# Attention with a linear memory, then an FFN: half-height causal masks for sequence 0, a parametric ReLU in the weight decode, ln(256) as the bias of the exponential, and three tiny preparation steps on ScalarE

## The chip, the cores and the metric

The kernel runs on one core of a Trainium2 chip (trn2). The metric is device time in microseconds (us): the median of the runs. Engines are named as in the profile: PE is TensorE's matmul stream and PEld its weight loads, DVE is VectorE, ACT is ScalarE, POOL is GpSimd, SP is SyncE, which issues the DMAs.

## What is computed

Eight sequences (B) of 576 tokens with eight heads of width 64 go through causal attention, which is mixed by a gate with a read from a per-head memory; the result, 4608 rows of 512, goes through a feed-forward block (FFN).

```python
scores = where(causal, -1e9, q @ k.T / sqrt(64));  a = exp(scores - scores.max(-1))
local  = (a / (a.sum(-1) + 1e-9)) @ v
q_p    = where(q > 0, q, exp(q) - 1) + 1
mem    = (q_p @ M_prev) / (q_p @ z_prev + 1e-6)
x      = sigmoid(beta) * mem + (1 - sigmoid(beta)) * local      # -> [4608, 512]
h      = x @ w_in                                               # w_in  [512, 2048], float64
out    = (h * clip(h + 3, 0, 6) / 6) @ w_out                    # w_out [2048, 512], float64
```

q, k, v, the memory and the gate are float32, both FFN weights float64.

## The kernel before

**Number formats.** From sequence 1 on every operand is split into two float16 parts (hi and lo), scaled by powers of two; a product is then three float16 matmuls (two for the scores, where the parts of k are stacked on the partitions). Sequence 0 and the first FFN block of 256 tokens have no time for that preparation and use float32 matmuls ("natural" operands, `nat`). The profile shows a float32 matmul as two passes.

**Attention.** A unit is one head and one group of 128-query blocks: block 0 and 1, block 2, block 3, or block 4 (64 rows). 256 units, eight sequences of 32. Scores stand with keys on the partitions in one PSUM bank. Per unit: the score products (L343 float32 for sequence 0, with the 64 dimensions of one head on 64 partitions: 0 to 63 for the first head of a pair, 64 to 127 for the second; L347 and L348 float16), and for the diagonal block one more product that adds the causal mask: identity (float16, 128 rows) times a matrix of 0 and -3e38 (L350). Then the maximum over key blocks (L360, or a copy on ACT, L358), the maximum over the partitions on POOL (L362), the subtraction on DVE (L368), the exponential on ACT (L377), and from sequence 1 on the float16 parts (L381 on POOL, L389 on DVE). Two units later come the products with v and with the memory (L407 and L408 in float32; L413 to L417), then their combination (L430 to L438).

L368 is a scalar_tensor_tensor: scores plus a shift, minus the maximum. The shift is such that the exponential comes out times 256. For sequence 0 it is a number, otherwise a column of 128 numbers (`scal[:, 1:2]`) read from SBUF.

**Preparation.** Ten steps per pair of heads (28 pairs, sequences 1 to 7) load q, k, v, find the largest sums of magnitudes (ACT L152, POOL L186), turn them into scales (`scale()`, L188 to L202, all of it on DVE) and split and stack the operands (ACT L156, DVE L157, DMAs).

**Weights.** The float64 words of the FFN weights are decoded by integer operations in 16 jobs of 128 x 1024 (L622 to L626): the upper word, read as float32 and scaled, goes through ACT; DVE shifts left by 3 (L623), puts the sign bit back from the upper word (L624), and adds three bits from the lower word (L625); ACT sums magnitudes. The first eight jobs are `w_in`, the rest `w_out`.

**FFN.** 18 blocks of 16 pieces: eight pieces of the first product (L523 to L525, float32 for block 0: L518), with the activation (L531 to L534), and eight of the second (L546 to L548, float32: L544). A piece is wanted at a time counted in pieces; attention is given priorities some pieces ahead. `nc` is built with a scheduler that orders all instructions of an engine by these priorities and by its own estimate of time. So the order on each engine is fixed when the program is built, and an edit of one step can move others.

Each engine runs its instructions in order; only the weight loads of PE go ahead.

Of the kernel before, what the change touches and what calls it, by code (L numbers as in the profile page):

```python
# [12 lines left out]
F32 = mybir.dt.float32  # L13
F16 = mybir.dt.float16
BF16 = mybir.dt.bfloat16
# [3 lines left out]
ALU = mybir.AluOpType  # L19
# [4 lines left out]
P = 128  # L24
EXP_BITS = 0x7F800000
TS = 14          # operands are scaled so that the largest sum of magnitudes along a row is in [2^TS, 2^(TS+1))
TF = 8           # weights are scaled so that the largest magnitude is in [2^TF, 2^(TF+1))
TG = 2.0 ** -9   # g is kept as TG * S * g
SA = 256.0       # exp() values are kept times SA
TINY = 2.0 ** -40  # L30
NSLOT = 6        # pairs of heads whose operands are on chip
NNAT = 1         # blocks of the FFN whose products are float32 ones
# the order of emission, in units of the attention, and the pieces of the FFN that things are wanted at
X_T = 10         # the first unit after which pieces of the FFN follow
SPL_K = 4        # parts of the second weights that are split per piece of the FFN
W_T = [9] * 8 + [10, 10, 11, 11, 12, 12, 13, 13]
PSS, PSO = 3, 2
# first loads: 0, 1 are the parts of a pair's q, k and v, 2 a job of the weights, 3 the memory
LOADS = ((0, 0), (3, 0), (0, 1), (0, 2), (0, 3), (2, 0), (2, 1), (1, 0), (1, 1), (2, 2), (1, 2), (1, 3), (2, 3))
B_T = (2, 3, 4, 5)  # L40
OF = (0,)        # query blocks of sequence 0 whose products stand in the FFN's banks
RMAX_STEPS = 3.0
LEAD = 40        # attention runs so many pieces of the FFN ahead
LEAD0 = 10
PO = 8           # preparation comes so many pieces after the unit that it is emitted at
XL = 12          # x comes so many pieces before the products that are emitted with it
DW = (-20, 2, 0, 1)      # decoding of the weights: first and step, for each of them
S1 = 8           # their splits
S2 = (16, 0.25)
TAIL = 80        # pieces of the FFN that are left to the end  # L50
HLB = 3
XPB = 4
# when the steps of preparing the pairs of the next sequence come, in units of this one
# [14 lines left out]
def kernel(ctx, tc, qT, kT, v, mz, beta, w_in, w_out, out):  # L68
    nc = tc.nc
    PE, DVE, ACT, POOL, SP = nc.tensor, nc.vector, nc.scalar, nc.gpsimd, nc.sync  # L70
    B, NP, _, S = qT.shape          # 8, 4, 128, 576
    H = 2 * NP
    D = 64
    NT, DM = out.shape              # 4608, 512
    DFF = w_in.shape[1]             # 2048
    NB = 5                          # 128-token tiles per sequence (the last one has 64)
    TB = 256                        # tokens of an FFN block
# [39 lines left out]
    for i in range(NSLOT):  # L117
        sizes = [2 * NB * P, 4 * S, 2 * S, NB * 2 * 129]
        whole = const.tile([P, sum(sizes) + 2], F16, name=f"slot{i}")
        at = 0  # L120
        for lst, n, pat, kw in zip((kst, qhl, qps, vst), sizes,
                                   ["p (h s) -> p h s", "p (x h s) -> p x h s", "p (h s) -> p h s",
                                    "p (t h e) -> p t h e"],
                                   [dict(h=2), dict(x=2, h=2), dict(h=2), dict(t=NB, h=2)]):
            lst.append(whole[:, at:at + n].rearrange(pat, **kw))
            at += n
        if i < NP:
            w32 = whole.bitcast(F32)
            nat.append(dict(q=w32[:, 0:S], k=w32[:, S:S + NB * P], qp=w32[:, S + NB * P:2 * S + NB * P],
                            v=w32[:, 2 * S + NB * P:2 * S + NB * P + NB * 130]  # L130
                            .rearrange("p (t h e) -> p t h e", t=NB, h=2)))
        else:
            raw.append(whole[:, 0:4096])

    def at(step):
        """what follows is wanted when so many pieces of the FFN are done"""
        tc.cur_priority = int(round(step * 1000))

    def scales(am, n, t, tag):
        """Power-of-two scales s, and 1/s, that bring each column's largest value to [2^t, 2^(t+1))."""  # L140
# [13 lines left out]
    def split(hi, lo, src, s):  # L154
        """hi + lo = src * s, both float16."""
# [4 lines left out]
    slots = {}  # L160

    def prep_steps(b, p):
# [25 lines left out]
        def scale():  # L188
            amr = st["amr"]
            DVE.tensor_scalar_add(amr[:, 3:4], amr[:, 0:1], 1.0)  # L190
# [4 lines left out]
            DVE.tensor_scalar(scal[:, 1:2], s[:, 0:1], s[:, 1:2], 8.0 * LN_SA, op0=ALU.mult, op1=ALU.mult)  # L195
            DVE.memset(scal[:, 2:3], SA * 1e-9)
            DVE.tensor_scalar(scal[:, 3:4], s[:, 3:4], 1e-6, mem[b]["s"][:, 1:2], op0=ALU.mult, op1=ALU.mult)
            coef = mem[b]["coef"][:, 2 * p:2 * p + 2]
            DVE.tensor_scalar_mul(coef[:, :, 0], omg[:, 2 * p:2 * p + 2], i[:, 2:3])
            eps = scal[:, 2:4].unsqueeze(1).broadcast_to([P, 2, 2])  # L200
            esc, shift = scal[:, 0:1], scal[:, 1:2]
            slots[b, p] = dict(sl=sl, esc=esc, shift=shift, coef=coef, eps=eps)  # L202
# [43 lines left out]
    def nat_load(p, part):  # L246
        """a pair of heads of sequence 0, for float32 products"""
# [12 lines left out]
    def nat_phi(p, part):  # L260
# [6 lines left out]
        slots[0, p] = dict(esc=0.125, shift=8.0 * LN_SA, coef=coef,  # L267
# [15 lines left out]
    def mem_steps(b):  # L283
# [16 lines left out]
        def conv():  # L300
# [7 lines left out]
            mem[b] = dict(t=t, s=s, coef=coef)  # L308
# [4 lines left out]
    # a unit: some 128-query blocks of one head, their scores in one PSUM bank, keys on partitions  # L313
# [4 lines left out]
    class Unit:  # L318
# [11 lines left out]
        def scores(self):  # L330
# [6 lines left out]
            for i, nq, c0, _ in self.blocks:  # L337
                q0 = i * P
                for j in range(i + 1):
# [9 lines left out]
                    if j == i:  # L349
# [14 lines left out]
        def sub(self):  # L364
            a = self.a = p2.tile([P, 512], F32, name=f"a_{self.id}", tag="a")
            for i, nq, c0, m0 in self.blocks:
                w = (i + 1) * nq
                DVE.scalar_tensor_tensor(  # L368
                    a[:, c0:c0 + w].rearrange("p (t q) -> p t q", q=nq),
                    self.sT[:, c0:c0 + w].rearrange("p (t q) -> p t q", q=nq),  # L370
                    slots[self.b, self.p]["shift"],
                    self.mb[:, m0:m0 + nq].unsqueeze(1).broadcast_to([P, i + 1, nq]),
                    op0=ALU.add, op1=ALU.subtract)

        def exp(self):
            a = self.a[:, 0:self.n]
            ACT.activation(a, a, AF.Exp, scale=slots[self.b, self.p]["esc"])  # L377
# [68 lines left out]
    # a block of TB tokens: the parts of x tiles that it holds  # L446
# [33 lines left out]
    def x_split(n, most):  # L480
        """float16 parts of x, for as many parts of block n as there are tiles for them"""
# [75 lines left out]
    ffn_pos = [0, 0]        # block, piece  # L557
    x_pos = [0, 0]          # next block to be transposed, its next step

    def x_step():  # L560
        """one step of bringing x of the next block into place; True when there was one to do"""
# [4 lines left out]
        free = n == fn or fk >= 8      # the tiles that the products of the block before read  # L566
# [32 lines left out]
    def w_raw(n):  # L599
        """where the words of job n stand: in the place of the other weights, or of what comes later"""  # L600
# [13 lines left out]
    def w_decode(n):  # L614
        """float64 chunks c and c + 1, as pairs of words, to float32 in chunks c + 1 and c + 2 of W"""
# [5 lines left out]
        # as a float32, the upper word has the upper 8 bits of the exponent, and the lower 3 in its fraction  # L621
        ACT.activation(m, hi.bitcast(F32), AF.Copy, scale=2.0 ** -112)  # L622
        DVE.tensor_single_scalar(d, d, 3, op=ALU.logical_shift_left)  # L623
        DVE.scalar_tensor_tensor(d, hi, -0x80000000, d, op0=ALU.bitwise_and, op1=ALU.bitwise_or)  # L624
# [36 lines left out]
    DVE.tensor_copy(negm, negf)  # L661
    DVE.memset(bias_g, TG / 2.0)
# [43 lines left out]
    def due(t):  # L706
        """the piece of the FFN that comes at the time of unit t"""
# [101 lines left out]
```

## Time and profile before

| | us |
|---|---|
| median of 3 runs | 1117.56 |
| fastest, slowest of the 3 | 1116.35, 1119.19 |
| span of the profiled execution | 1120.2 |
| PE busy in it | 1083.2 |
| DVE busy | 930.7 |
| ACT busy | 791.1 |
| POOL busy | 412.2 |

The profiled execution is a further one; the page gives its span, from its first to its last instruction, and no other time for it. The span is 2.6 us above the median and 1.0 above the slowest of the three.

How to read it: a group row has the line, engine and operation, out<-in, shapes and count, then busy us and mean ns of one, then the idle time of the engine just before them and what ended it. A timeline row has its start, how long it took, engine, line, operation, and how many were merged. Matmuls overlap in their pipeline, so a row's length is a latency; the time that one occupies PE is the distance between starts.

### The profile page before, as it was taken

Reading aid. Unit: us, or ns where it says so; the run is one execution under the profiler, and the core shown is the slowest. Engines: PE = TensorE matmul, PEld = TensorE weight load, DVE = VectorE, ACT = ScalarE, POOL = GpSimd, SP = SyncE. Lnnn points to the kernel's source line nnn. Section 1 sums busy time; section 2 is a strip of 40 time slices with the busy share of each in tenths; the row PEclk is TensorE's granted clock in tenths of the full one; section 3 lists DMA queues with packets and bytes.
Section 4 is the critical chain, followed back from the end, with each engine's and each line's share of the span. In section 5 each row is a group of like instructions: output and inputs, shape, how many; then the busy total and the mean of one; then the engine's idle time right before and its main releaser. Section 6 shows DMA issues by size and latency. Waiting matters only on the chain.

```text
span 1120.2 us, 28768 instructions
## 1 busy us (share of the span) xinstructions
PE 1083.2 (97%) x10736; PEld 797.4 (71%) x10736; DVE 930.7 (83%) x2436; ACT 791.1 (71%) x1880; POOL 412.2 (37%) x544
## 2 busy tenths in 40 slices
PE   8999999999999899999999999999999999999998
PEld 6888767586767667676768576867685868685664
DVE  5999889899899969998999988888799968893321
ACT  5787879677877778787877787668686857563321
POOL 3322223444444433554244533354344433341000
PEclk9999999999999999999999999999999999999999
DMA  8734452333424343315332434233404230101100
GB/s 263 291 100 160 119 135 70 94 91 87 116 84 106 70 118 89 97 45 138 97 76 71 101 96 102 76 92 97 116 22 107 77 69 14 36 5 36 27 13 19
DMA packets 101468, 101.39 MB, mean 91 GB/s; under 512 B 50256, under 2 KB 80976, under 8 KB 101328
## 3 DMA queue, kind: packets, MB, share of 16 engines
q1 hardware_dynamic: 101328, 99.56, 33.1%
q8 instruction: 84, 1.38, 0.5%
q14 instruction: 56, 0.46, 0.1%
HBM read 48.14 MB, written 9.44 MB: 51 GB/s over the span
## 4 chain that ended last, share of the span: by engine, by line
PE 42%; DVE 32%; ACT 8%; issue 8%; DMA 6%; POOL 2%; SPq 1%; DVEq 0%; ACTq 0%; POOLq 0%
DVE a L368 6%; PE po L546 5%; PE po L548 5%; PE po L547 5%; PE ph L523 5%; DVE rm L360 5%; PE ph L524 4%; PE ph L525 4%; DVE al L389 4%; DVE r L532 3%; PE ph L518 3%; DVE g L534 2%; PE sT L343 2%; DVE W L157 2%; POOL mb L362 2%
## 5 line engine op out<-in xcount | busy, mean ns | idle before, releaser
L362 POOL PARTITION_ALL_REDUCE mb<-rm x256 | 251.7, 983 | 336.7 <-DVE rm L360 237.4
L523 PE MATMUL ph<-x,W 128*128 128x256 f16 x1088 | 297.6, 274 | 12.7 <-DVE r L532 7.3
L525 PE MATMUL ph<-x,W 128*128 128x256 f16 x1088 | 297.5, 273 | 0.0
L524 PE MATMUL ph<-x,W 128*128 128x256 f16 x1088 | 297.4, 273 | 0.0
L381 POOL TENSOR_SCALAR_AFFINE_SELECT ah<-a 128x384 f16<-128x384 f32 (+2 forms) x224 | 145.4, 650 | 214.4 <-ACT a L377 105.4
L546 PE MATMUL po<-W,g 128*128 128x512 f16 x544 | 206.6, 380 | 1.9 <-ACT ot L554 1.6
L548 PE MATMUL po<-W,g 128*128 128x512 f16 x544 | 206.5, 380 | 0.8 <-DVE g L534 0.8
L547 PE MATMUL po<-W,g 128*128 128x512 f16 x544 | 206.7, 380 | 0.0
L377 ACT ACTIVATE a<-a,scal 128x384 f32<-128x384 f32 (+2 forms) x224 | 141.6, 633 | 57.0 <-DVE a L368 48.8
L368 DVE SCALAR_TENSOR_TENSOR a<-sT,scal,mb 128x128 f32<-128x128 f32 (+4 forms) x280 | 147.2, 541 | 13.3 <-POOL mb L362 12.4
L360 DVE TENSOR_REDUCE rm<-sT 128x128 f32<-128x256 f32 (+3 forms) x256 | 135.6, 530 | 11.5 <-PE sT L350 4.6
L389 DVE TENSOR_TENSOR al<-a,ah 128x384 f16<-128x384 f32 (+2 forms) x224 | 134.0, 598 | 9.2 <-POOL ah L381 8.0
L532 DVE SCALAR_TENSOR_TENSOR r<-r,ph 128x512 f32<-128x512 f32 x136 | 92.1, 677 | 53.2 <-ACT r L531 52.6
L436 ACT ACTIVATE x<-o,cf 128x64 f32<-128x64 f32 (+1 forms) x320 | 100.6, 314 | 44.2 <-DVE cf L432 39.5
L531 ACT ACTIVATE r<-ph,bias_g,gsc 128x512 f32<-128x512 f32 x136 | 106.5, 783 | 34.2 <-PE ph L525 29.1
L347 PE MATMUL sT<-slot 128*128 128x128 f16 (+1 forms) x840 | 123.7, 210 | 3.9 <-DVE a L368 2.1
L348 PE MATMUL sT<-slot 128*128 128x128 f16 (+1 forms) x840 | 124.3, 210 | 0.0
L523 PEld LDWEIGHTS <-W 128*128 128x128 f16 x1088 | 106.8, 98 | 23.1 <-issue 6.6
L413 PE MATMUL o<-slot,ah 128*128 128x65 f16 (+1 forms) x840 | 116.3, 195 | 6.9 <-ACT y L437 3.6
L533 ACT ACTIVATE g<-r 128x512 f16<-128x512 f32 x136 | 86.4, 636 | 51.2 <-DVE r L532 51.1
L524 PEld LDWEIGHTS <-W 128*128 128x128 f16 x1088 | 106.7, 98 | 19.5 <-issue 5.0
L414 PE MATMUL o<-slot,ah 128*128 128x64 f16 (+1 forms) x840 | 115.4, 195 | 0.0
(149 smaller groups left out, 2387.4 us busy)
## 6 DMA issues: line engine op xcount, KB each, us to landing
slot<-q SPq DMA_DIRECT2D x112, 144.0 KB, 2.5
out<-ot SPq DMA_DIRECT2D x36, 256.0 KB, 2.0
stv<-vn SPq DMA_DIRECT2D x28, 320.0 KB, 3.3
W<-w_in SPq DMA_DIRECT2D x8, 1024.0 KB, 9.5
slot<-w_out SPq DMA_DIRECT2D x8, 1024.0 KB, 4.9
stq<-qT SPq DMA_DIRECT2D x28, 288.0 KB, 3.1
stk<-kT SPq DMA_DIRECT2D x28, 288.0 KB, 3.3
slot<-k SPq DMA_DIRECT2D x112, 72.0 KB, 2.0
```

The source lines that it names most:

```text
L360: DVE.tensor_reduce(rm[:, m0:m0 + nq], src.rearrange("p (t q) -> p q t", q=nq), axis=AX.X, op=ALU.max)
L362: POOL.partition_all_reduce(mb[:, 0:self.m], rm[:, 0:self.m], P, RMAX)
L368: DVE.scalar_tensor_tensor(a[:, c0:c0 + w].rearrange("p (t q) -> p t q", q=nq), self.sT[:, c0:c0 + w].rearrange("p (t q) -> p t q", q=nq), ...
L377: ACT.activation(a, a, AF.Exp, scale=slots[self.b, self.p]["esc"])
L381: POOL.affine_select(self.ah[:, 0:self.n], a, pattern=[[0, self.n]], compare_op=ALU.is_ge, fill=0.0, base=1, channel_multiplier=0)
L389: DVE.tensor_tensor(self.al[:, 0:n], self.a[:, 0:n], self.ah[:, 0:n], op=ALU.subtract)
L523: PE.matmul(ph[:, m], wh, f["xh"][:, c], start=c == 0, stop=False)
L524: PE.matmul(ph[:, m], wh, f["xl"][:, c], start=False, stop=False)
L525: PE.matmul(ph[:, m], wl, f["xh"][:, c], start=False, stop=c == 3)
L546: PE.matmul(po, gh[:, m, ts], W2[:, m, 0:512], start=m == 0, stop=False)
L547: PE.matmul(po, gh[:, m, ts], W2[:, m, 512:], start=False, stop=False)
L548: PE.matmul(po, gl[:, m, ts], W2[:, m, 0:512], start=False, stop=m == 15)
```

## The change

Comments are dropped as well, so lines move: what was L343, L350, L368, L377 and L624 to L625 stands in the new file at L349, L357, L378, L385 and L633 (the old L624 is gone). Five things change:

1. **Masks of sequence 0.** In place of one product of 128 rows and 128 columns there are two (one in the 64-row block) of 64 rows and 64 columns, on the same 64 partitions as the head's score products. Their operands, `selm` and `neg2`, lie in the unused end of an operand slot and are built at the start by some 15 small DVE instructions. Sequences 1 to 7 keep the old mask.
2. **Subtraction.** L368 becomes a tensor_tensor: scores minus maximum, without the shift.
3. **Exponential.** ln(256) is the bias of the activation. In the built program the bias was the number 0.0 and is the number 5.545; no operand is added.
4. **Decode.** Instead of a copy the activation is a parametric ReLU whose slope for negative inputs is -2^32: after the shift left by 3 the sign bit is then in place, and L624 goes.
5. **Tiny steps.** Of the nine instructions of `scale()` on 1 to 4 columns, one goes (the shift), and three move from DVE to ACT: q's sum plus 1, the scaled epsilon, and a coefficient. A column `eps1` per sequence is added (DVE).

```diff
+            selm = free[:, 0:2 * P].rearrange("p (a k) -> p a k", a=2)
+            neg2 = free[:, 2 * P:3 * P].rearrange("p (a q) -> p a q", a=2)
...
         def scale():
-            DVE.tensor_scalar_add(amr[:, 3:4], amr[:, 0:1], 1.0)
+            ACT.activation(amr[:, 3:4], amr[:, 0:1], AF.Copy, bias=1.0)
             s, i = scales(amr, 4, TS, f"{b}_{p}")
...
-            DVE.tensor_scalar(scal[:, 1:2], s[:, 0:1], s[:, 1:2], 8.0 * LN_SA, op0=ALU.mult, op1=ALU.mult)
             DVE.memset(scal[:, 2:3], SA * 1e-9)
-            DVE.tensor_scalar(scal[:, 3:4], s[:, 3:4], 1e-6, mem[b]["s"][:, 1:2], op0=ALU.mult, op1=ALU.mult)
+            ACT.activation(scal[:, 3:4], s[:, 3:4], AF.Copy, scale=mem[b]["eps1"])
-            DVE.tensor_scalar_mul(coef[:, :, 0], omg[:, 2 * p:2 * p + 2], i[:, 2:3])
+            ACT.activation(coef[:, :, 0], omg[:, 2 * p:2 * p + 2], AF.Copy, scale=i[:, 2:3])
...
-                    if j == i:
+                    if j == i and self.b == 0:
+                        for a in range(nq // D):
+                            PE.matmul(o[:, a * D:(a + 1) * D], selm[r, a, :], neg2[r, a, :],
+                                      start=False, stop=a == nq // D - 1)
+                    elif j == i:
                         PE.matmul(o, ident16, negm[:, 0:nq], start=False, stop=True)
...
-                DVE.scalar_tensor_tensor(
+                DVE.tensor_tensor(
                     a[:, c0:c0 + w].rearrange("p (t q) -> p t q", q=nq),
                     self.sT[:, c0:c0 + w].rearrange("p (t q) -> p t q", q=nq),
-                    slots[self.b, self.p]["shift"],
-                    self.mb[:, m0:m0 + nq].unsqueeze(1).broadcast_to([P, i + 1, nq]),
-                    op0=ALU.add, op1=ALU.subtract)
+                    self.mb[:, m0:m0 + nq].unsqueeze(1).broadcast_to([P, i + 1, nq]), op=ALU.subtract)
...
-            ACT.activation(a, a, AF.Exp, scale=slots[self.b, self.p]["esc"])
+            ACT.activation(a, a, AF.Exp, scale=slots[self.b, self.p]["esc"], bias=LN_SA)
...
-        ACT.activation(m, hi.bitcast(F32), AF.Copy, scale=2.0 ** -112)
+        ACT.activation(m, hi.bitcast(F32), AF.Prelu, scale=2.0 ** -112, alpha=-2.0 ** 32)
         DVE.tensor_single_scalar(d, d, 3, op=ALU.logical_shift_left)
-        DVE.scalar_tensor_tensor(d, hi, -0x80000000, d, op0=ALU.bitwise_and, op1=ALU.bitwise_or)
         DVE.scalar_tensor_tensor(d, lo, 29, d, op0=ALU.logical_shift_right, op1=ALU.bitwise_or)
```

The scheduler makes another order of it on every engine. Three places follow. First PE at the start of the program, the scores of sequence 0, heads 0 and 1 of the first pair; `sT` is a unit's PSUM bank (sequence, group, pair and head are left out of some names, a number at the end counts buffers), `slot_102` that pair's q and k, `ident` and `negm` the mask's operands. Before:

```order
L343 MATMUL sT_0_0_0_191<-slot_102 128x128
L350 LDWEIGHTS ident_89
L350 MATMUL sT_0_0_0_191<-negm,ident_89 128x128
L343 MATMUL sT_0_0_0_191<-slot_102 128x128 x2
L350 LDWEIGHTS ident_89
L350 MATMUL sT_0_0_0_191<-negm,ident_89 128x128
L343 MATMUL sT_0_0_1_206<-slot_102 128x128
```

And now, with `slot_105` for the place of `selm` and `neg2`:

```order
L349 MATMUL sT_0_0_0_206<-slot_102 128x128
L357 LDWEIGHTS slot_105
L357 MATMUL sT_0_0_0_206<-slot_105 128x64
L357 LDWEIGHTS slot_105
L357 MATMUL sT_0_0_0_206<-slot_105 128x64
L349 MATMUL sT_0_0_0_206<-slot_102 128x128 x2
L357 LDWEIGHTS slot_105
L357 MATMUL sT_0_0_0_206<-slot_105 128x64
L357 LDWEIGHTS slot_105
L357 MATMUL sT_0_0_0_206<-slot_105 128x64
L349 MATMUL sT_0_0_1_223<-slot_102 128x128
```

The units stand in the same order; each mask has become two weight loads and two products of half the columns. Over the whole order the masks of sequence 0 are 40 products before and 72 now, and PE changes between 64-row and 128-row products 97 times before and 63 times now.

Second DVE, the second decode job and the attention around it; `W_95` holds the decoded words, `W_96` the raw ones, `cf`, `rm`, `a` and `slot` belong to attention. Before:

```order
L430 TENSOR_TENSOR cf_0_0_1_0_285<-o_0_0_0_0_237,nat_eps 128x4
L625 SCALAR_TENSOR_TENSOR W_95<-W_96,W_95 128x1024
L623 TENSOR_SCALAR W_95<-W_95 128x1024
L430 TENSOR_TENSOR cf_0_0_1_1_296<-o_0_0_0_1_240,nat_eps 128x4
L431 RECIPROCAL cf_0_0_1_0_285<-cf_0_0_1_0_285 128x4
L265 SCALAR_TENSOR_TENSOR slot_102<-slot_102 128x320
L624 SCALAR_TENSOR_TENSOR W_95<-W_96,W_95 128x1024
L431 RECIPROCAL cf_0_0_1_1_296<-cf_0_0_1_1_296 128x4
```

And now:

```order
L438 TENSOR_TENSOR cf_0_0_1_0_310<-o_0_0_0_0_258,nat_eps 128x4
L632 TENSOR_SCALAR W_95<-W_95 128x1024
L439 RECIPROCAL cf_0_0_1_0_310<-cf_0_0_1_0_310 128x4
L438 TENSOR_TENSOR cf_0_0_1_1_321<-o_0_0_0_1_261,nat_eps 128x4
L633 SCALAR_TENSOR_TENSOR W_95<-W_96,W_95 128x1024
L440 TENSOR_TENSOR cf_0_0_1_0_310<-cf_0_0_1_0_310,coef_161 128x4
```

A job is two DVE instructions instead of three, and the small steps of attention (`cf`) stand behind one long instruction less.

Third the scales of pair 0 of sequence 1. On DVE before (`amr` are the reduced sums, `i` and `s` the scales, `wi` belongs to the weights):

```order
L144 TENSOR_SCALAR i_0_694<-i_0_694 128x4
L143 TENSOR_SCALAR i_wi<-wm_i 128x1
L145 RECIPROCAL s_0_693<-i_0_694 128x4
L194 SCALAR_TENSOR_TENSOR scal_0_698<-i_0_694 128x1
L199 TENSOR_SCALAR coef_262<-omg,i_0_694 128x2
L196 MEMSET scal_1_959 128x1
L195 TENSOR_SCALAR scal_0_698<-s_0_693 128x1
L197 TENSOR_SCALAR scal_0_698<-s_0_693,s_m_252 128x1
```

And now on ACT, with attention (`a`, `r`) and the weights (`W`, and `slot_106` and `slot_107` as their scratch) between:

```order
L195 ACTIVATE amr_0_674<-amr_0_674 128x1
L385 ACTIVATE a_1_3_0_833<-a_1_3_0_833 128x384
L631 ACTIVATE W_96<-slot_107 128x1024
L634 ACTIVATE slot_106,am_190<-W_96 128x1024
L385 ACTIVATE a_1_3_1_878<-a_1_3_1_878 128x384
L536 ACTIVATE r_2_713<-ph_2_704,half 128x512
L161 ACTIVATE W_95<-W_95,ws_i 128x512
L203 ACTIVATE coef_283<-omg,i_0_718 128x2
L634 ACTIVATE slot_107,am_190<-W_96 128x1024
```

The first step, `amr`, now runs on ACT between POOL's reduction and DVE's first step; the coefficient comes seven ACT instructions later, and the split of k, which before was the first ACT instruction to need the scales, seven after that.

More of the change, by code (lines that the diff above doesn't have):

```diff
@@ L133 @@
             raw.append(whole[:, 0:4096])
+        if i == NP - 1:
+            free = whole.bitcast(BF16)[:, 2 * (2 * S + NB * P + NB * 130):]
+            selm = free[:, 0:2 * P].rearrange("p (a k) -> p a k", a=2)
+            neg2 = free[:, 2 * P:3 * P].rearrange("p (a q) -> p a q", a=2)
     def at(step):
@@ L194, in scale @@
             DVE.scalar_tensor_tensor(scal[:, 0:1], i[:, 0:1], 0.125, i[:, 1:2], op0=ALU.mult, op1=ALU.mult)
[L195 removed]
             DVE.memset(scal[:, 2:3], SA * 1e-9)
[L197 removed]
+            ACT.activation(scal[:, 3:4], s[:, 3:4], AF.Copy, scale=mem[b]["eps1"])
             coef = mem[b]["coef"][:, 2 * p:2 * p + 2]
[L199 removed]
+            ACT.activation(coef[:, :, 0], omg[:, 2 * p:2 * p + 2], AF.Copy, scale=i[:, 2:3])
             eps = scal[:, 2:4].unsqueeze(1).broadcast_to([P, 2, 2])
[L201 to L202 removed]
+            esc = scal[:, 0:1]
+            slots[b, p] = dict(sl=sl, esc=esc, coef=coef, eps=eps)
         def pair_tiles(nm):
@@ L266, in nat_phi @@
         coef = mem[0]["coef"][:, 2 * p:2 * p + 2]
-        slots[0, p] = dict(esc=0.125, shift=8.0 * LN_SA, coef=coef,
+        slots[0, p] = dict(esc=0.125, coef=coef,
                            eps=nat_eps.unsqueeze(1).broadcast_to([P, 2, 2]))
@@ L307, in conv @@
             DVE.tensor_scalar(coef[:, :, 1], gate, s[:, 1:2], i[:, 0:1], op0=ALU.mult, op1=ALU.mult)
-            mem[b] = dict(t=t, s=s, coef=coef)
+            eps1 = small.tile([P, 1], F32, name=f"eps1_{b}", tag="eps1", bufs=2)
+            DVE.tensor_scalar_mul(eps1, s[:, 1:2], 1e-6)
+            mem[b] = dict(t=t, s=s, coef=coef, eps1=eps1)
         return [load, lambda: None, absmax, conv]
@@ L661 @@
     DVE.tensor_copy(negm, negf)
+    DVE.memset(selm, 0.0)
+    for r in (slice(0, D), slice(D, P)):
+        DVE.tensor_copy(selm[r, 0, 0:D], ident[r, r])
+        DVE.tensor_copy(selm[r, 1, D:P], ident[r, r])
+        r0 = slice(r.start, r.start + 1)
+        DVE.memset(selm[r0, 0, 0:1], 0.0)
+        DVE.memset(selm[r0, 0, D:P], 1.0)
+        for a in range(2):
+            DVE.tensor_copy(neg2[r, a, :], negf[r, r])
+        DVE.memset(neg2[r0, 0, :], -3e38)
     DVE.memset(bias_g, TG / 2.0)
```

## Prediction

> **What bounds the kernel now.** I read the page's totals first, then the busy time in slices of 28 us, the waits of PE, and the chain that ended last.
>
> ```profile
> PE 1083.2 (97%) x10736; PEld 797.4 (71%) x10736; DVE 930.7 (83%) x2436; ACT 791.1 (71%) x1880; POOL 412.2 (37%) x544
> ```
>
> PE is busy for 97% of the span of 1120.2 us; only some 37 us are left in which it is idle. The slices say where (columns: stretch, its length, then busy us of PE, PEld, DVE, ACT and POOL, then the granted clock and DMA):
>
> ```profile
> 0.00:28.00 28.00, 23.14 (x90) 18.47 (x90) 16.52 (x57) 15.45 (x34) 9.56 (x15) 1.00 0.89 263
> 28.00:56.00 28.00, 27.21 (x117) 24.18 (x118) 25.30 (x63) 21.86 (x60) 10.09 (x9) 1.00 0.80 291
> 56.00:84.00 28.00, 27.87 (x134) 23.16 (x132) 27.43 (x61) 23.80 (x52) 7.37 (x8) 1.00 0.32 100
> 84.00:112.00 28.00, 28.00 (x165) 23.42 (x164) 26.11 (x46) 21.59 (x46) 6.24 (x7) 1.00 0.45 159
> 224.00:252.00 28.00, 26.16 (x355) 22.99 (x352) 27.93 (x63) 21.86 (x53) 13.90 (x17) 1.00 0.36 92
> 364.00:392.00 28.00, 24.42 (x302) 18.05 (x300) 28.00 (x74) 20.95 (x47) 12.09 (x18) 0.99 0.32 70
> ```
>
> Three regimes: up to 84 us PE and DVE are both nearly full with few matmuls (x117 in a slice against x355 later); then PE is full; later PE loses 1.8 us (at 224) or 3.6 us (at 364) of a slice in which DVE is full. What PE waits for in all (us, times, longest):
>
> ```profile
> PE ph L523 <- DVE r L532: 7.3, 7, 2.5
> PE ph L523 <- DMA x<-W: 5.2, 4, 2.3
> PE sT L343 <- DMA slot<-qT: 4.6, 1, 4.6
> PE o L413 <- ACT y L437: 3.6, 6, 1.3
> PE o L413 <- POOL ah L381: 3.2, 4, 1.3
> PE sT L347 <- DVE a L368: 2.1, 5, 0.7
> ...
> PE sT L347 <- DVE cf L430: 1.5, 1, 1.5
> ...
> PE o L415 <- DVE al L389: 1.2, 3, 0.5
> ```
>
> Where DVE is relieved, only such waits can be won; where PE is full, only work of PE itself. Of the chain of waits, the part from 26 to 66 us:
>
> ```profile
> by line: DVE W L624 18.4%; issue 11.8%; DVE W L625 11.4%; DVE a L368 7.5%; DVE W L623 6.3%; POOL mb L362 6.0%; ACT W L622 5.1%; DVE rm L360 4.9%; ACT x L436 4.7%; PE sT L343 4.1%; ACT y L437 3.8%; DVE cf L432 3.1%; ACT a L377 3.1%; DVE mz L
> ```
>
> The decode leads it: L624, which goes, is 18.4% of 40 us, 7.4 us. But PE is idle in 28 to 84 us for only 0.8 + 0.1 us. Two chains of about the same length run side by side, so each has to become shorter for the end to move.
>
> **The masks.** PE's first unit, with starts from the timeline of PE (start, us, line, shape; a start less the next one's is the time occupied):
>
> ```profile
> 5.29 0.29 PE L350 MATMUL sT<-negm,ident 128*128 128x128 bf16 x1
> 5.51 0.58 PE L343 MATMUL sT<-slot 64*128 64x128 f32 x1
> ...
> 5.88 0.63 PE L343 MATMUL sT<-slot 64*128 64x128 f32 x2
> ...
> 6.31 0.42 PE L343 MATMUL sT<-slot 64*128 64x128 f32 x1
> 6.66 0.29 PE L350 MATMUL sT<-negm,ident 128*128 128x128 bf16 x1
> ```
>
> The two float32 passes over 64 rows from 5.88 to 6.31 take 0.21 each. The last one before the 128-row mask takes 0.35 (6.31 to 6.66), the mask 0.22 (5.29 to 5.51), the first pass behind it 0.37 (5.51 to 5.88): 0.94 us. Where a 128-row float32 product follows the mask there is no such step:
>
> ```profile
> 39.78 0.29 PE L350 MATMUL sT<-negm,ident 128*128 128x128 bf16 x1
> 39.86 0.42 PE L407 MATMUL o<-slot,a 128*128 128x65 f32 x1
> ```
>
> The mask then takes 0.08, although the type changes as well; so the rest looks like the price of changing between 64 and 128 rows. With the halves on the same 64 rows the three steps become 0.21, two halves, and 0.21. No row shows a 64-row product of 64 bf16 columns. From below each half takes 0.05 (somewhat under the 0.08 of the whole mask), from above 0.21 like a float32 pass. The sum is 0.52 to 0.84, the saving 0.10 to 0.42. I take the middle, 0.25, because a float32 weight load has to fit behind the second half. Eight masks stand within a unit of block 0 and 1, one per head, and six more are followed by the next unit's scores before 80 us, by the order of before: 14 x 0.25 = 3.5 us (1.4 to 5.9). Of the other 26 most are followed by 128 rows: there the change of rows only moves from ahead of the mask to behind it: 0, at most 26 x 0.1 (half of the 0.22) = 2.6 either way. The 15 DVE instructions that build the operands lie in the 4.6 us in which PE waits for q, in a slice where DVE is loaded least (16.5 of 28 us): 0; what they cost without that cover follows below.
>
> The Trainium skill, "TensorE: Matmul & The Clock Gate", section "Why this matters for your kernels", says that a product with few rows takes as long as one with 128, and that a gain comes only from products that run on different rows at once. By it the halves, which follow each other on the same rows, win nothing, and the 32 products more are a loss. It knows no price for the change of rows, which the 0.35, 0.22 and 0.37 show; a rival below goes by it.
>
> **The decode and the early stretch.**
>
> ```profile
> L624 DVE SCALAR_TENSOR_TENSOR W<-W,W 128x1024 int32<-128x1024 int32 x8 | 9.7, 1215 | 0.0
> L624 DVE SCALAR_TENSOR_TENSOR W<-slot,W 128x1024 int32<-128x1024 int32 x8 | 9.7, 1207 | 0.0
> L622 ACT ACTIVATE W<-W 128x1024 f32<-128x1024 f32 x8 | 9.2, 1154 | 4.5 <-DMA W<-w_in 4.5
> ```
>
> 9.7 + 9.7 = 19.4 us of DVE go. The activation replaces a copy of the same shape, 1154 ns; a parametric ReLU is not in the trace, and I take the same (at worst a second pass, 1.15 more, on ACT, which has 4 to 6 us free per slice). By itself this buys PE's idle 0.9 us; its worth is that DVE keeps up with a PE that needs 3.5 us less.
>
> There is a third effect. The granted clock reads 1.00 in all these slices, but PE's rows say otherwise:
>
> ```profile
> 56.70 2.02 PE L518 MATMUL ph<-x,W 128*128 128x256 f32 x4
> 58.66 1.65 PE L343 MATMUL sT<-slot 64*128 64x128 f32 x6
> ...
> 64.50 1.65 PE L343 MATMUL sT<-slot 64*128 64x128 f32 x6
> ```
>
> ```profile
> 66.36 7.08 PE ph L518 x22
> ...
> 76.81 3.51 PE ph L518 x16
> ```
>
> Four passes of the first FFN block take 1.96 at 56.7 (0.49 each), sixteen take 3.51 at 76.8 (0.22 each). PE ran at about half speed until somewhere in the long run of 22 passes at 66.4 us. In the new order this run of FFN products starts one unit's scores earlier (the 1.65 at 64.50 now stand behind it), so these run at full speed and cost 0.8 less. Early stretch: 3.5 + 0.9 + 0.8 = 5.2 us, from 1 to 10.
>
> The same page, section "Part 1: The HAM clock gate", has the half clock as the state of a PE that has not been busy for a window of 3.4 us, with windows that run freely; by it the moment could shift by an estimated 1.7 us at half effect, within the range above.
>
> **Subtraction and tiny steps.**
>
> ```profile
> L368 DVE SCALAR_TENSOR_TENSOR a<-sT,scal,mb 128x512 f32<-128x512 f32 x56 | 41.5, 740 | 2.4 <-POOL mb L362 2.2
> L368 DVE SCALAR_TENSOR_TENSOR a<-sT,mb 128x512 f32<-128x512 f32 x8 | 5.5, 684 | 1.1 <-PE o L407 1.1
> L534 DVE TENSOR_TENSOR g<-r,g 128x512 f16<-128x512 f32 x136 | 100.1, 736 | 15.1 <-ACT g L533 14.9
> L195 DVE TENSOR_SCALAR scal<-s 128x1 f32<-128x1 f32 x28 | 5.6, 199 | 0.0
> L197 DVE TENSOR_SCALAR scal<-s,s_m 128x1 f32<-128x1 f32 x28 | 5.6, 200 | 0.0
> L199 DVE TENSOR_SCALAR coef<-omg,i 128x2 f32<-128x2 f32 x28 | 7.5, 268 | 0.0
> L190 DVE TENSOR_SCALAR amr<-amr 128x1 f32<-128x1 f32 x28 | 4.1, 145 | 3.8 <-POOL amr L186 3.8
> L156 ACT ACTIVATE mz<-stm,s_m 128x8 f16<-128x8 f32 x7 | 2.4, 343 | 0.0
> L669 ACT ACTIVATE gate<-beta_sb 128x8 f32<-128x8 f32 x1 | 0.2, 208 | 1.6 <-DMA beta_sb<-beta 1.6
> ```
>
> The column operand costs 740 - 684 = 56 ns. A tensor_tensor on PSUM in this size is not shown; the nearest is L534 at 736, from SBUF to float16, so the saving lies between 4 and 56, and I take 56, since the number form reads the same two tensors. Over 280 instructions 16 us of DVE, 40 per sequence or 2.2 us. The tiny steps take 4.1 + 5.6 + 5.6 + 7.5 = 22.8 us off DVE, 3.3 per sequence, and add 208 + 2 x 343 ns = 0.9 us per pair to ACT, 25 us in all on 791: ACT has the room. The bias replaces a number by a number: nothing.
>
> At L190's 145 ns the 15 instructions for the masks' operands would cost 2.2 us.
>
> So over the seven later sequences DVE loses 7 x 5.5 = 38 of its 930.7 us. PE's waits behind DVE (7.3 + 2.1 + 1.5 + 1.2), and behind ACT and POOL steps that DVE feeds (3.6 + 3.2), are 19 us; I let a quarter go, 5 us, and take back 2 for the detours through ACT: 3 us. The scheduler deals all of these waits anew, so this term may come out between 6 lost and 9 won.
>
> **Sum.** 5.2 + 3 = 8.2 us. Against the profiled span of 1120.2 that is 1112.0; the unprofiled median lies 2.6 lower, so I forecast 1117.6 - 8.2 = 1109.4 us. About 0.3%, 3.4 us, can be told from no change.
>
> **Rivals.**
> - *The step at the masks is not one of rows.* If it belongs to every mask product, 32 more of them at 0.22 cost 7 us and the 3.5 are not won: 1117.6 + 7 - 0.9 - 0.8 - 3 = 1120 us. That would bear out the page's rule named above. Against it speaks the 0.08 ahead of L407. 8%.
> - *Preparation comes late* (the other side). In the new order ACT holds the first and the last tiny step of a pair, with some 14 instructions from the one to the split of k; at ACT's mean (791.1 us over x1880, 0.42) that is 5.9 us. Once a pair's q and k land after PE reaches its scores, PE waits. With 1.5 us lost in each of seven sequences and the early gain kept: 1117.6 + 10.5 - 5.2 = 1123 us. It decides when the slack of a pair is under 5.9 us. Against it: no wait of PE for a stacked operand stands in the list of waits. 8%.
> - *The new order eats the gain*: the waits of 19 us grow by as much as the early stretch wins; within 3.4 us of 1117.6. 14%.
> - *PE reaches full speed much earlier*, since the passes at the masks become denser. If it did at 40 us instead of about 70, the work between would take half: 15 us less, 5.2 of them counted already, so about 1100 us. Against it: PE was all but full from 28 to 56 us and stayed slow. 8%.
>
> My forecast has the remaining 62%. Faster by over 3.4 us: 62 + 8 and 2 of the third rival's 14, 0.72. Within: the third's other 12 and 5 of the first's 8, 0.17. Slower: 8 and the first's other 3, 0.11. The range reaches from the early full speed (1100, less 1 for the later stretch) to the first rival's 1120, which takes in 5.2 + 3 with both bounds, 1 - 6 to 10 + 9, but for their joint ends; the late preparation is left out.
>
> **What would show it.** Right: the mask halves at 0.05 to 0.2 from start to start with passes of 0.21 around them; the 16 passes at 0.22 beginning 4 to 8 us earlier than 76.8; L624 gone from the chain; PE's waits behind DVE below 12 us. Wrong: passes of 0.37 behind the half masks; a list of PE's waits with the preparation's DMAs in it; or PE's waits, with the early stretch shorter, as large as before.

## The result, and the profile after

| | before | after |
|---|---|---|
| median of 6 runs each, same chip | 1119.72 | 1114.31 |
| lowest, highest | 1116.35, 1122.92 | 1113.58, 1114.74 |
| span of the profiled execution | 1120.2 | 1111.9 |

The changed kernel is 5.4 us faster: the ratio is 0.9949, 95% interval 0.9935 to 0.9964. The forecast was 1109.4, which was 8.2 less than the 1117.56 of the first three runs of before. Before's median over six runs is 2.2 us higher than that, so 2 of the 5 us by which the forecast is too low are the base, and 3 are gain that did not come. Later measurements gave before medians of 1120 to 1121. In the two profiled executions the spans differ by 8.3; the medians count.

The page's totals of after, and four of the slices shown of before (stretch, length, busy us of PE, PEld, DVE, ACT, POOL, granted clock, DMA):

```profile
PE 1077.7 (97%) x10768; PEld 795.1 (72%) x10768; DVE 890.5 (80%) x2330; ACT 802.5 (72%) x1964; POOL 399.7 (36%) x544
```

```profile
0.00:28.00 28.00, 20.72 (x107) 19.18 (x107) 15.18 (x72) 16.36 (x41) 7.47 (x15) 1.00 0.87 255
28.00:56.00 28.00, 27.74 (x122) 24.49 (x121) 21.66 (x64) 22.34 (x58) 8.70 (x9) 1.00 0.83 290
56.00:84.00 28.00, 28.00 (x151) 24.32 (x151) 23.28 (x53) 24.00 (x56) 8.40 (x9) 1.00 0.43 150
364.00:392.00 28.00, 28.00 (x358) 20.53 (x355) 26.28 (x69) 23.63 (x58) 10.97 (x19) 1.00 0.47 111
```

DVE has its relief: 40 us less in all, and 21.7 and 23.3 in the slices where it had 25.3 and 27.4. But in the first slice PE is busy for 20.7 us where it was 23.1: it stands idle more than before. PE's list of waits in after:

```profile
PE sT L349 <- DMA slot<-qT: 4.6, 1, 4.6
PE o L423 <- DVE al L397: 4.4, 12, 0.7
PE ph L531 <- DVE r L540: 4.2, 7, 1.2
PE sT L353 <- DVE a L378: 3.0, 4, 1.6
PE sT L349 <- DVE a L378: 3.0, 3, 2.4
PE o L421 <- POOL ah L389: 2.4, 6, 0.9
...
```

Behind DVE these are 14.6 us, against 12.1 before: not fewer. The new one is the L349 row, 2.4 us long, in the early stretch.

To see where the 8.3 us between the two traces arise I counted PE's work: along PE's order, a fixed weight for each product (0.109 us for 256 float16 columns, its spacing at full speed; 0.213 for a float32 pass of 128 columns, its spacing at half speed, where full speed gives 0.112; and so on), masks left out, 1009.3 us in either kernel. It serves as a ruler only. The table has the time at which so much of it was done:

```
work done, us      15     35     40    100    150    400    700   1008
before           32.5   65.5   73.1  133.2  185.1  463.9  793.4 1115.0
after            31.9   65.1   70.1  128.2  183.2  458.4  783.8 1106.8
difference       -0.6   -0.4   -3.0   -5.0   -1.9   -5.5   -9.7   -8.3
```

At 65 us, with most masks of the early stretch done, after is 0.4 us ahead; from 40 us on it was between 0.4 and 1.5 ahead. It wins 2.6 in the next 5 us, then gains and gives back in places.

### The profile page after: what moved, and what is told of

The parts are those of the page before. It is cut to its first block, busy times and chain, and to the rows that moved or that the text cites. A ratio compares the mean times of both kernels' runs of the same rounds, so it can differ in the third digit from the quotient of the medians.

```text
span 1111.9 us, 28866 instructions
## 1 busy us (share of the span) xinstructions
PE 1077.7 (97%) x10768; PEld 795.1 (72%) x10768; DVE 890.5 (80%) x2330; ACT 802.5 (72%) x1964; POOL 399.7 (36%) x544
## 5 line engine op out<-in xcount | busy, mean ns | idle before, releaser
L372 POOL PARTITION_ALL_REDUCE mb<-rm x256 | 249.1, 973 | 335.8 <-DVE rm L370 247.1
L389 POOL TENSOR_SCALAR_AFFINE_SELECT ah<-a 128x384 f16<-128x384 f32 (+2 forms) x224 | 135.9, 610 | 208.6 <-ACT a L385 89.0
L385 ACT ACTIVATE a<-a,scal 128x384 f32<-128x384 f32 (+2 forms) x224 | 141.4, 632 | 53.5 <-DVE a L378 43.9
L378 DVE TENSOR_TENSOR a<-sT,mb 128x128 f32<-128x128 f32 (+3 forms) x320 | 148.3, 479 | 19.6 <-POOL mb L372 15.2
L397 DVE TENSOR_TENSOR al<-a,ah 128x384 f16<-128x384 f32 (+2 forms) x224 | 137.2, 613 | 11.7 <-POOL ah L389 10.8
L353 PE MATMUL sT<-slot 128*128 128x128 f16 (+1 forms) x840 | 126.3, 211 | 3.0 <-DVE a L378 3.0
L354 PE MATMUL sT<-slot 128*128 128x128 f16 (+1 forms) x840 | 127.8, 210 | 0.0
L531 PEld LDWEIGHTS <-W 128*128 128x128 f16 x1088 | 106.7, 98 | 19.4 <-issue 2.3
L532 PEld LDWEIGHTS <-W 128*128 128x128 f16 x1088 | 106.6, 98 | 19.3 <-issue 4.2
L533 PEld LDWEIGHTS <-W 128*128 128x128 f16 x1088 | 106.6, 98 | 12.2
```

Source lines behind the costliest of these rows:

```text
L353: PE.matmul(o, kk, qhl[sl][:, 0, h, q0:q0 + nq], start=True, stop=False)
L354: PE.matmul(o, kk, qhl[sl][:, 1, h, q0:q0 + nq], start=False, stop=j < i)
L372: POOL.partition_all_reduce(mb[:, 0:self.m], rm[:, 0:self.m], P, RMAX)
L378: DVE.tensor_tensor(a[:, c0:c0 + w].rearrange("p (t q) -> p t q", q=nq), self.sT[:, c0:c0 + w].rearrange("p (t q) -> p t q", q=nq), self.m ...
L397: DVE.tensor_tensor(self.al[:, 0:n], self.a[:, 0:n], self.ah[:, 0:n], op=ALU.subtract)
L531: PE.matmul(ph[:, m], wh, f["xh"][:, c], start=c == 0, stop=False)
```

## The experiments

**The parts, each alone on the kernel before**, measured together on one chip. e1 has the new masks, e2 the new decode, e3 the subtraction without shift and the bias, e4 the three steps on ACT, each as in the diff above.

> The kernel before with the half-height masks alone. By the terms of the prediction: 1.4 to 5.9 us less, most of it before 84 us; each mask step inside a unit at 0.3 to 0.6 us where it was 0.94. By the rival that the clock decides: PE's full speed begins earlier than the 70.8 us of before, and the gain is what the work between takes less; up to that moment the masks themselves win under 1 us, since the chain of DVE, POOL and ACT beside PE is no shorter. By the rival that the newly dealt order decides: anywhere within 4 us of before, with the difference arising after 170 us.

> The kernel before with the parametric ReLU in the decode alone (one of three DVE instructions of a job gone, 19.4 us of DVE). By the prediction: PE's 0.9 us of idle time between 28 and 84 us, so under 1 us in all, since PE itself has as much work as before. By the rival that DVE's chain bounded the early stretch: 2 to 4 us less, with PE denser up to 84 us. By the rival of the order: within 4 us either way, arising after 170 us.

> The kernel before with the subtraction as a tensor_tensor, without the shift, and with the bias of the exponential. By the prediction: DVE loses 280 x 56 ns = 16 us and 5.6 us of the shift, 22 us in all, of which a share like the quarter taken for the waits comes out: 1 to 3 us less, spread over the sequences from 170 us on; nothing before 84 us. By the rival of the order: within 4 us either way, in a few places and not spread.

> The kernel before with the three tiny steps of the scales on ACT alone (17.2 us off DVE, some 22 us onto ACT: 28 x (203 + 301 + 302) ns by the changed kernel's rows). By the prediction: between 1 us less (DVE's relief) and 2 us more (detours through ACT). By the rival that the preparation comes late: 5 us more or worse, with waits of PE for a pair's stacked operands in its list. By the rival of the order: within 4 us either way.

| | median | ratio to before, 95% | mean granted clock | lost to it, us |
|---|---|---|---|---|
| before (18 runs) | 1121.06 | | 0.9965 | 3.9 |
| e1 masks | 1114.55 | 0.9944 (0.9923 to 0.9965) | 0.9988 | 1.3 |
| e2 decode | 1121.01 | 1.0000 (0.9984 to 1.0016) | 0.9952 | 5.4 |
| e3 subtraction | 1113.18 | 0.9940 (0.9918 to 0.9961) | 0.9984 | 1.8 |
| e4 tiny steps | 1131.52 | 1.0089 (1.0073 to 1.0106) | 0.9918 | 9.2 |

(The clock is the mean over a kernel's runs, for before over all its 69 runs beside these experiments; what is lost is one minus it, times the time. It sees only what comes after PE first reached full speed.) The decode is worth nothing alone, as forecast. The others move the time by 6.5, 7.9 and 10.5 us, more than any of their costs, and they do not add up: four parts together give 5.4. By the same count of work e1 and e3 are ahead of before by 0.2 and 0.5 us at work 35 and by 5.0 and 6.5 at work 250; e4 is 0.6 ahead at 35 and 8.5 behind at 300. Most of the differences arise between 130 and 360 us, behind nearly all the masks.

**A control, and the changed kernel without one part.** e5 is the kernel before with one small instruction issued twice; it gives the scheduler something to deal anew, and nothing else.

```diff
             DVE.memset(scal[:, 2:3], SA * 1e-9)
+            DVE.memset(scal[:, 2:3], SA * 1e-9)
```

> The kernel before with one small DVE instruction of each pair's scales issued twice (a memset of one column, 28 instructions of about 60 ns, 1.7 us of DVE in all): a control that gives the scheduler a reason for another order and nothing else. If single parts moved the time by their own cost, this one is 0 to 1.7 us slower. If the newly dealt order is what moved it (the parts alone gave -6.3, 0, -7.9 and +10.5 us, most of which arose between 130 and 400 us), this one lies anywhere within some 5 us of before, and the difference arises in the same stretch, as idle time of PE and as stretches of half clock.

It measured 1125.69 against 1120.37, ratio 1.0048 (1.0030 to 1.0067): 5.3 us slower from 28 instructions that take 1.7 us on an engine with room. So a new order alone moves this kernel by 3.6 us or more, nearly as much as the whole change does.

e6 takes the three tiny steps back to DVE (the diff's lines of `scale()` undone), e7 takes back the masks.

> The changed kernel with the three tiny steps back on DVE. If the steps on ACT cost what they cost alone (10.5 us beside the kernel before), this one is about 10 us faster than the changed kernel, near 1105 us. If that 10.5 us belonged to the order, it lies within 5 us of the changed kernel, on either side. By the prediction, which had these steps at 1 us won to 2 us lost: within 2 us of it.

e6: 1115.03, ratio 0.9953 (0.9939 to 0.9967). The 10.5 us that the steps cost alone are not to be won back here: they belonged to the order in which e4 was dealt, 5.3 of them in half-clock time by the table above.

> The changed kernel with the old masks of 128 rows in sequence 0. By the prediction's term the masks are worth 3.5 us (1.4 to 5.9): it is that much slower than the changed kernel, and its PE needs some 3 us more for the score passes before 65 us. By the theory that another chain bounds PE up to 65 us: PE's passes take these 3 us longer and its idle time there is 2 to 3 us shorter, so that at 65 us it stands within 1 us of the changed kernel; what remains is the moment of full speed and the order.

e7: 1118.35, ratio 0.9971 (0.9957 to 0.9986), some 2.5 us slower than after by the ratios, whose intervals overlap; this lies within the prediction's term. It ran at a mean clock of 0.9948, which by itself loses 2.1 us more than after's 0.9967. In its trace, at work 35, it stands at 64.4 us, 0.7 ahead of after, with the dearer masks; between work 10 and 30 it is 0.1 to 0.6 behind.

**Rows against count.** e10 is the kernel before with two halves per mask, but over 128 rows. PE has the same order of products as in e1; what differs is the price at the masks, and the 15 small DVE instructions that build e1's operands.

```diff
-                        PE.matmul(o, ident16, negm[:, 0:nq], start=False, stop=True)
+                        for a in range(nq // D):
+                            PE.matmul(o[:, a * D:(a + 1) * D], ident16, negm[:, a * D:(a + 1) * D],
+                                      start=False, stop=a == nq // D - 1)
```

> The kernel before with each mask of sequence 0 as two products of 128 rows and 64 columns: as many products as in the changed kernel, but over 128 rows. If the price at a mask is the change between 64 and 128 rows: the pass ahead of a mask stays at 0.35 and the first behind it at 0.37 us, and the whole step is 0.9 to 1.05 us. If it is a matter of the count or the width of the mask products: the passes around it fall to 0.21 as in the changed kernel.

The pass ahead of a mask stays at 0.350 us from start to start, the first behind it at 0.375: it is the rows and not the count or the width of the mask products. Then the surprise: its one run took 1114.37, e1's median is 1114.55. As far as one run can tell, nearly all of e1's 6.5 us belong to its order and not to the rows of its masks. One row of each over the same 60 us, first e1, then e10:

```profile
5.00:65.00 60.00, 56.25 (x263) 50.76 (x263) 49.23 (x116) 43.40 (x108) 19.19 (x15) 1.00 0.75 250
```

```profile
5.00:65.00 60.00, 59.31 (x262) 50.31 (x262) 48.91 (x110) 43.27 (x108) 19.10 (x15) 1.00 0.76 251
```

With 64-row masks PE works 3.06 us less for the same products (x263, x262), and stands idle 3.06 us more. The masks' saving has about the size forecast, and at 65 us PE is no further on.

**What PE waits for instead.** The timeline of after around 20 us (start, us, engine, line):

```profile
13.64 0.79 PE L349 MATMUL sT<-slot 64*128 64x128 f32 x2
14.23 0.31 PE L357 MATMUL sT<-slot 64*128 64x64 bf16 x2
14.35 1.20 PE L349 MATMUL sT<-slot 64*128 64x128 f32 x4
15.35 0.31 PE L357 MATMUL sT<-slot 64*128 64x64 bf16 x2
15.59 0.69 PE L415 MATMUL o<-slot,a 128*128 128x65 f32 x2
...
16.63 1.13 ACT L631 ACTIVATE W<-W 128x1024 f32<-128x1024 f32 x1 [2.95 <-DMA W<-w_in]
...
17.80 0.69 DVE L632 TENSOR_SCALAR W<-W 128x1024 int32<-128x1024 int32 x1 [4.33 <-ACT W L631]
18.52 1.23 DVE L633 SCALAR_TENSOR_TENSOR W<-W,W 128x1024 int32<-128x1024 int32 x1
...
19.66 0.61 DVE L378 TENSOR_TENSOR a<-sT,mb 128x128 f32<-128x128 f32 x2
...
20.43 0.76 PE L349 MATMUL sT<-slot 64*128 64x128 f32 x2 [2.44 <-DVE a L378]
```

And the same place in before:

```profile
17.73 0.69 DVE L623 TENSOR_SCALAR W<-W 128x1024 int32<-128x1024 int32 x1 [4.55 <-ACT W L622]
18.46 1.23 DVE L624 SCALAR_TENSOR_TENSOR W<-W,W 128x1024 int32<-128x1024 int32 x1
...
19.60 0.62 DVE L368 SCALAR_TENSOR_TENSOR a<-sT,mb 128x128 f32<-128x128 f32 x2
...
19.85 0.63 PE L408 MATMUL o<-m_nat,slot 128*128 128x65 f32 x2
...
20.41 0.79 PE L343 MATMUL sT<-slot 64*128 64x128 f32 x2
```

The first words of w_in land at 16.6 us. ACT, and behind it DVE for 4.3 us, stand at the head of their queues for them, with the third unit's subtraction behind. In before PE was still at work when that subtraction came; now PE is there earlier and waits. The same scores begin at 20.43, and began at 20.41. By the count of work after is 2.6 us ahead just ahead of this wait (7 us of work, done at 14.7 us) and 0.2 behind it (10 us, done at 22.6). e9 takes away what makes it wait: w_in's first load comes two places later, so that the decode stands behind that subtraction on both engines.

```diff
-LOADS = ((0, 0), (3, 0), (0, 1), (0, 2), (0, 3), (2, 0), (2, 1), (1, 0), (1, 1), (2, 2), (1, 2), (1, 3), (2, 3))
+LOADS = ((0, 0), (3, 0), (0, 1), (0, 2), (0, 3), (1, 0), (1, 1), (2, 0), (2, 1), (2, 2), (1, 2), (1, 3), (2, 3))
```

> The changed kernel with the first load of w_in two places later in the list of first loads, so that on ACT and DVE the first decode job stands behind the subtraction and the exponential of the third unit and not ahead of them. By the theory that the masks' 3 us were given back because DVE stood 4.3 us at the head of its queue for a decode whose words had not landed: PE's wait of 2.4 us at 20.4 us goes, the same scores begin at about 18 us, and PE stands 1.5 to 2.5 us ahead of the changed kernel until 50 us. By the rival that the third unit is late for another reason (its own loads, or POOL): those scores begin within 0.5 us of 20.4 as before. The total can go either way by the order, within 5 us.

```profile
17.92 0.79 PE L349 MATMUL sT<-slot 64*128 64x128 f32 x2
...
20.84 0.69 DVE L632 TENSOR_SCALAR W<-W 128x1024 int32<-128x1024 int32 x1 [2.25 <-ACT W L631]
```

The scores begin at 17.92, and PE stands 2.2 us ahead of after at work 15, and 0.2 to 1.7 between 20 and 35. So it is shown that this wait takes the gain at 20 us; what takes part of it again further on was not looked for. As a kernel e9 is worse, 1129.47, ratio 1.0097 (1.0064 to 1.0131): the rest was dealt anew and loses far more than 2 us.

**The clock.** e8 puts 14 products of 512 columns ahead of everything, over 128 rows; e11 the same over 64 rows (a 64 in place of P in the slices of `gh`). Nobody reads their result.

```diff
+    DVE.memset(gh[:, 0:2, :], 1.0)
+    wps = ps_f.tile([P, 2, TB], F32, name="wps", tag="h")
+    for k in range(14):
+        PE.matmul(wps, gh[0:P, 0, 0:P], gh[0:P, 0:2, :], start=True, stop=True)
```

> The changed kernel with 14 products of 128 rows by 512 columns at the very start, of ones, into a bank that nobody reads: 6 us of dense work, some 2.5 us of it after the first scores could have begun. If any busy stretch of 3 to 7 us brings PE to full speed and the work of sequence 0 keeps it there, the passes of the early stretch take 0.11 to 0.12 from some 7 us on, and the time falls by 5 to 20 us as far as the DVE and DMA chains allow. If the 64-row float32 work does not count as busy, PE falls back to half speed within 4 to 8 us and full speed returns at the long run of FFN products as before: 0 to 3 us slower.

> The changed kernel with 14 products of 512 columns at the very start as before, but over 64 rows in place of 128. The 128-row ones brought PE to full speed at 5.6 us, for 6.8 us. If what counts is how much of the array works, 64 rows do not do it: no full speed before some 65 to 71 us. If only time in which a matmul streams counts, full speed comes at about 5 to 8 us as with 128 rows, and the slow early stretch is due to gaps between the float32 products and not to their rows.

These products in e8, then in e11 (shortest, median and longest in ns; first and last start):

```profile
L667 PE MATMUL wps<-g x14: 379/634/634, 1.5 to 6.3; 128*128 128x512 f16 x14
```

```profile
L667 PE MATMUL wps<-g x14: 606/631/631, 1.5 to 7.0; 64*128 64x512 f16 x14
```

Over 128 rows the last ones run at full speed, over 64 none does. What follows in e8, by stretch (the last three numbers are granted clock, DMA share, GB/s):

```profile
5.70:12.40 6.70, 3.14 (x35) 2.31 (x33) 2.19 (x9) 2.94 (x8) 1.07 (x1) 1.00 0.84 198
12.50:70.30 57.80, 55.86 (x244) 50.25 (x245) 43.30 (x115) 46.67 (x116) 19.19 (x17) 0.50 0.77 263
70.50:118.20 47.70, 47.70 (x315) 41.11 (x314) 42.67 (x99) 42.48 (x92) 11.03 (x13) 1.00 0.47 146
```

Full speed lasts for 6.8 us and comes back at 70.4, with the run of FFN products, although PE is busy for 55.9 of the 57.8 us between. So the early stretch is slow because sequence 0's work does not hold the clock up, and it cannot be warmed once for all. All twelve runs of e8 have a mean clock between 0.967 and 0.974, which fits the same course. e8 measured 1119.24, ratio 0.9991 (0.9975 to 1.0008), about 5 us slower than after; e11 in its one run 1132.83, full speed from 77.9 us. That the rows are what counts for these 14 products rests on e11's single run of some 6 us of dense work; where these 6 us lie against windows of 3.4 us (see the last section) could also decide, and was not tested. Nor need it be the rows alone that keep the stretch slow: of e8's 244 products from 12.5 to 70.3 us 78 are score passes over 64 rows and 112 are passes of 65 columns over 128 rows.

**The same order, the old price.** e12 is the changed kernel with its halves over 128 rows, as in e10. All instructions stand in the same order as in after, on every engine.

> The changed kernel with its mask halves over 128 rows (identity times mask, 64 columns each) in place of 64: as many products, and the same order of instructions on every engine, so that only the price at the masks differs. By the prediction's term: 1.4 to 5.9 us slower than the changed kernel. By the theory that the 3 us of PE at the masks only turn into idle time up to 65 us: score passes at 0.29 us on average in place of 0.24, idle time before 65 us some 2.5 us shorter, and PE at 65 us within 1 us of the changed kernel; the total then differs only by the moment of full speed: 0 if it stays near 67 us, 2 to 3 us slower if it comes at some 70 us as in the kernels with the old price.

Between work 10 and 30 it is 0.2 to 0.8 us behind after (56.9 against 56.7 us at 30): in this order too most of the masks' saving is idle time. Then its trace parts from that of after. PE in after:

```profile
54.25 1.92 PE L526 MATMUL ph<-x,W 128*128 128x256 f32 x4
56.10 1.65 PE L349 MATMUL sT<-slot 64*128 64x128 f32 x6
...
63.34 5.83 PE L526 MATMUL ph<-x,W 128*128 128x256 f32 x18
```

And in e12:

```profile
54.84 1.82 PE L526 MATMUL ph<-x,W 128*128 128x256 f32 x4
56.59 0.93 PE L349 MATMUL sT<-slot 64*128 64x128 f32 x6
...
61.29 4.15 PE L526 MATMUL ph<-x,W 128*128 128x256 f32 x18 [0.61 <-ACT x L516]
```

At the end of four FFN passes e12 comes to full speed, at 56.4 us (six score passes then take 0.93 and not 1.65); in after the same four, 0.6 us earlier, are not followed by it, and full speed comes at 66.8. Later e12 pays. Two stretches of it:

```profile
121.20:124.70 3.50, 3.50 (x28) 3.17 (x27) 2.72 (x8) 3.41 (x11) 0.38 (x1) 1.00 0.53 166
124.70:128.10 3.40, 3.40 (x21) 3.02 (x21) 1.88 (x7) 2.44 (x8) 0.94 (x1) 0.50 0.00 0
```

From 124.7 to 145.2 the granted clock is 0.50 although PE is busy throughout, much of the time with score passes of 64 rows and 64 columns (50 of them between 117.8 and 145.2); after has 70 of them in the same time and a granted clock of 1.00. Why the clock fell in e12 is open. Its twelve runs lie between 1114.06 and 1125.92, median 1118.66, ratio 0.9989 (0.9969 to 1.0009), some 4.5 us slower than after by the ratios: within the prediction's 1.4 to 5.9, and more than the 0 to 3 of the other theory. 3.2 of these are clock (6.9 us lost against 3.7), and its four runs at a clock of 0.996 or 0.997 average 1115.3, near after's 1114.31. Whether the cheaper masks make after keep the clock more often, or its six runs were lucky, stays open.

## Why the prediction was right in sign and range, and too hopeful

**The masks' price: right in size, partly by luck.** Forecast 3.5 us (14 times 0.25); e1 against e10: 3.06 in PE. It is made up otherwise than forecast: the pass ahead of the mask falls from 0.350 to 0.213 and both halves take 0.12 (14.23 to 14.35 above), but the first pass behind them still takes 0.354, not 0.21 (with three of 0.213 it makes the 1.00 from 14.35 to 15.35). So the step is 0.69 us, down from 0.94. Only the part ahead of the mask and the mask itself were a matter of rows. The eight steps within a unit make 2.0 us. That the sum comes so near is partly luck, for the prediction left something out: where no 128-row product stands between two units, the last passes of one and the first of the next run side by side on different 64 rows, with starts 5 or 6 ns apart. This happens four times each in e1 and after, two of them before 65 us, and never in before, e10 or e12, whose masks have 128 rows. From the first pass behind the second unit's inner mask to that behind the third's it is 2.31 us in e10 and 1.29 in e1, 1.03 less, where the forecast has two steps of 0.25.

**What it buys: wrong in the traces, and this is the step that failed.** The prediction said that the worth of the decode's relief was "that DVE keeps up with a PE that needs 3.5 us less". DVE was not short of time there. It stood 4.3 us for a DMA at the head of its queue, and a removed instruction does not shorten that. At 65 us 0.4 us were left of 3.5 + 0.9 (0.4 to 1.5 from 40 us on). The trace of before had the row, DVE's 4.55 us of waiting at 17.73; PE arrived just as the subtraction behind it ended, so nothing named it. In whole kernels the picture is less plain: with the same order, e12 is 4.5 us slower than after, as the price would have it, but most of that is clock, and e10's one run is as fast as e1.

**Full speed earlier: the right mechanism, at the wrong size.** 0.8 us forecast; in these two traces it is the 2.6 between work 35 and 40 (70.8 to 66.8 us). But it is no fixed property of the order: with after's order it came at 66.8 and 56.4, and over all traces at 56.4 to 77.9.

**The later stretch: the number came, the reason did not.** Forecast 3 us, from waits behind DVE growing shorter; the traces show 3.3 from work 100 to the end; the medians leave 0.4 for it, if the early 5.0 hold in every run. PE's waits behind DVE went from 12.1 to 14.6, where I had named under 12 as the sign. e5 and e4 show that orders differ by 5 to 10 us there for reasons with no price in the diff.

**The small prices held.** Groups of after (mean ns behind the comma):

```profile
L378 DVE TENSOR_TENSOR a<-sT,mb 128x512 f32<-128x512 f32 x64 | 43.4, 679 | 4.4 <-POOL mb L372 3.5 <-PE o L415 0.7
L631 ACT ACTIVATE W<-W 128x1024 f32<-128x1024 f32 x8 | 9.1, 1134 | 4.3 <-DMA W<-w_in 4.3
L195 ACT ACTIVATE amr<-amr 128x1 f32<-128x1 f32 x28 | 5.7, 203 | 1.5 <-POOL amr L191 1.5
L201 ACT ACTIVATE scal<-s,eps 128x1 f32<-128x1 f32 x28 | 8.4, 301 | 1.6 <-DVE s L150 1.6
L203 ACT ACTIVATE coef<-omg,i 128x2 f32<-128x2 f32 x28 | 8.4, 302 | 10.2 <-DVE i L149 10.0
```

The subtraction fell by 740 - 679 = 61 ns (56 forecast); the parametric ReLU costs what the copy did (1134 against 1154); the tiny steps cost ACT 203 + 301 + 302 = 0.81 us per pair (0.9). DVE's instructions, their lengths added up, fell by 57 us (19.4 + 38 forecast); its busy time, which counts overlapping ones once, fell by 40.

**The rivals.** That the price is one of every mask product fell with e10. Late preparation did not happen: no wait of PE for a stacked operand stands in after's list, and e6 gains nothing from undoing the detour. "The new order eats the gain" was too narrow: the order decides most of the total, either way.

So the 5.4 us are real for this program, and are not the sum of its edits' costs. Shown are 3.06 us of PE that turn into idle time, and the wait at 20 us that takes most of what PE has won by then; in the traces the rest is the moment of full speed and the idle and half-clock time of another order. Not shown is what the cheaper masks do to the clock, and so what they are worth in the medians.

## What to carry to other kernels

Where a scheduler deals the order, measure a neutral edit first: here one of 1.7 us moved the time by 5.3, and an edit's own price is only told by a pair of kernels with the same order (e1 and e10, after and e12). Before a busy engine is relieved, look at what its supplier waits for just before they meet: a wait of 4.5 us that ends as PE arrives costs nothing, until PE saves time ahead of it; then it takes what PE saves. And what is put at the head of two in-order queues for a DMA holds up everything behind it, however little either engine has to do.

## What the runs showed of the hardware

- Full speed comes and goes by windows. In before the granted clock is 0.50 for 3.4 us in two places; the stretch ahead of the first and that stretch:

```profile
388.30:391.70 3.40, 1.05 (x9) 0.81 (x9) 3.40 (x11) 2.25 (x7) 1.55 (x3) 1.00 0.83 173
391.70:395.10 3.40, 3.40 (x15) 1.69 (x13) 0.33 (x3) 2.19 (x8) 0.00 (x0) 0.50 0.71 221
```

  PE had been busy for 1.05 of 3.4 us. So a stretch in which PE stands still for some 2 us costs up to 1.7 us more afterwards. About half of the variance between before's 69 runs goes with the mean clock: its runs at a mean clock of 1.000 average 1118.1 us (4 runs), those at 0.994 average 1123.2 (8 runs). The Trainium skill, "TensorE: Matmul & The Clock Gate", section "Part 1: The HAM clock gate", has such windows of 3.4 us that run freely, and these rows agree; that one order reached full speed at 66.8 us in after and at 56.4 in e12 fits windows that do not start with the program.
- By the same section of the Trainium skill a window of sustained activity lifts the throttle. Here PE's busy time alone did not: 57.8 us with PE 97% busy at 0.50 in e8, on passes over 64 rows and passes of 65 columns, and 20.5 us with PE always busy at 0.50 in e12. In e11's one run 64-row products stayed slow where e8's 128-row ones did not. What counts as activity is not settled by these runs.
- Score passes of the two heads of a pair, on different 64 rows, can start 6 ns apart (5.822 and 5.828 us in after) where passes on the same rows start 213 apart at half speed.
